# Another order table for an attention and feed-forward kernel on one core

## The chip, the cores and the metric

The kernel runs on one core of a Trainium2 chip. Five instruction streams run side by side: TensorE (PE in the profile, with its weight loads as PEld) for matrix products, VectorE (DVE), ScalarE (ACT) and GpSimd (POOL) for elementwise work, and SyncE (SP), which here only issues DMAs; POOL issues DMAs too, and ACT three. Each stream works through its instructions in the order in which they were built, and waits at an instruction until what it depends on is done. The metric is the device time of one execution in microseconds, and the time of a kernel is the median over its runs.

## What is computed

64 heads (8 batches of 8), 576 positions of 64 values, attention by feature maps, then a feed-forward layer that takes the largest of three products:

```python
def phi(x):
    proj = np.einsum('bhsd,df->bhsf', x, w_phi)
    proj = proj - np.max(np.abs(proj), axis=-1, keepdims=True)
    return np.concatenate([np.exp(proj), np.exp(-proj)], axis=-1)
q_p, k_p = (phi(q), phi(k))
kv = np.einsum('bhsf,bhsd->bhfd', k_p, v)
z = np.sum(k_p, axis=2)
num = np.einsum('bhsf,bhfd->bhsd', q_p, kv)
den = np.einsum('bhsf,bhf->bhs', q_p, z)[..., None] + 1e-06
x = (num / den)                                  # heads side by side: 4608 rows of 512
h = np.maximum(np.maximum(x @ w1, x @ w2), x @ w3)   # 768 wide
out = h @ w_out
```

## The kernel before

The attention is cut into 16 units of four heads, the feed-forward layer into nine chunks: one per batch (512 rows each), and a ninth for the 64 last positions of all batches.

A unit goes through these steps. Queries and keys are loaded and cast by POOL's DMAs into `qk_bf` (four buffers), the last positions of the queries by SP's into `tail_raw`, the values by SP's into `v_raw` (four buffers, which the first keys and, at the end, partial sums use as well). The loads become transposed blocks in `qkT`: for units 0 to 3 on TensorE (`tps`, L508, copied out by DVE or ACT at L519 and L521), from unit 4 on by two DMA transposes on SP (L527), one for the keys and one for the queries. TensorE projects: `psk`, `pst` and `psq` (L545) for the maxima, which DVE takes (L549), `psm` (L642, and L650 for the last positions) for the queries' exponentials. ACT makes the exponentials `Ek` (L553) and `Eq` (L633). From the keys' maxima ACT makes `em` (L591), and POOL multiplies the values with it into `vab` (L597), about 2 us a product and two to a unit. TensorE forms `kvps` from `Ek` and `vab` (L616), 72 products a unit (for units 0 and 1 in two halves of 36), and `psn` (L683); DVE scales and adds (L692, L695), takes reciprocals (L740), POOL divides into `x_sb` (L741), and a DMA transpose on SP (L773) turns that into `xT` (units 0 and 1 on TensorE).

The weights w1, w2, w3 and w_out are loaded by four DMAs on POOL's queue (L952). TensorE transposes w1 into `pwT` (L1008) and multiplies it with w_out (`pm`, L1018); POOL subtracts w1 from w2 and w3 in six steps (L982). A chunk then has the products `ups` (L891), the comparisons on DVE (L901) and ACT (L905), and the products `ops` (L924, L929), copied out by ACT or DVE (L939) and stored by SP (L943). Chunks 6 to 8 use a form with seven products instead of eight (`ups` at L820, sums on DVE at L829 and L864). One piece of chunk 7 is stored in two parts, of 384 and of 128 columns, by ACT.

All of this is made as 1687 steps, each with its dependencies and buffers. Which step stands where is not found by the program: the string `PLAN` lists all steps, in the order in which they are built. A word such as `262S0@42.1` names the step (262), its engine (T for TensorE, D, A, G for POOL, S for SyncE), the buffer of its tile among those of its kind, if it takes one (0), and a start in microseconds. The order of the words is what counts. No engine waits for the start that stands in a word; before 30 us `fill` uses it for one thing: where the listed starts leave TensorE a gap, it puts products of no use (`idler`, L1066) into it, as many as fit beside the uses of the PSUM banks. For a step that two engines can do, such as a copy, the letter also decides which does it.

```python
for word in PLAN.split():
    what, start = word.split("@")
    at = next(i for i, c in enumerate(what) if c.isalpha())
    n, slots = nodes[int(what[:at])], iter(what[at + 1:])
    n.eng, n.start = ENGINES[what[at]], float(start)
    ...
    order.append(n)
```

Of the kernel before, what the change touches and what calls it, by code (L numbers as in the profile page):

```python
# [90 lines left out]
103G0@1.2 3A@0.7 1D@0.8 4A@1.3 10S0@0.7 12D1@4.0 11A@4.0 5D@4.2 0G@1.9 19T0@4.5 20A0@4.9 6D@4.4 29T12@5.5 32D0@6.0 9G@2.5 8G@3.2  # L91
35D@6.6 31A0@6.8 102G@3.9 260G2@4.6 16S0@1.1 104G@8.1 17G@8.3 186G3@8.6 185G@9.3 259G@10.0 1166G@10.7 13S@2.5 7A@7.2 106T3@7.4 33A0@7.5
34A@8.0 30A@8.4 107D1@8.1 119T45@8.8 122D1@9.3 187S1@2.9 124A1@9.2 123A1@9.7 112T67@9.1 115D@9.9 110T0@9.4 111A@10.2 114A@10.6
120A@11.1 121A@11.6 25T2@10.0 15D@10.5 14D@10.7 27T1@10.9 21T3@11.1 118D@10.9 26D@11.5 28D@11.8 43T04@12.2 73T21@12.3 22D@12.0
23T3@12.7 125D@12.4 113A@12.1 46D@13.0 47D0@13.3 18S1@4.3 24D@13.6 116A@12.6 76A0@13.0 45A@13.5 1169G@11.5 54A0@13.8 75A0@14.0
117A@14.4 1167G@12.2 74A@14.9 36T56@13.1 108T4@13.8 42D@14.0 39D@14.6 109D@15.2 38A@15.4 77A@15.9 41A@16.4 58A@16.8 51T37@15.1 52D@15.8
44A@17.0 126T24@15.9 130D1@16.4 105S2@5.0 131T13@16.5 333G1@13.6 129D@16.7 53D@17.0 133D@17.6 57G0@14.3 55G@14.5 2G@15.6 56G@15.8
188G@16.9 128A@17.3 37A@17.6 137A1@18.0 40A@18.2 78T0@17.5 62T47@17.8 80A@18.7 64A0@19.0 132D@18.2 48T35@18.4 50D@18.8 63D@19.4
49D@19.6 60G@17.2 61G@18.3 138G1@18.4 59G@19.5 127A@19.1 79A@19.4 68T67@19.3 134T15@19.6 263T4@19.9 190T3@20.4 135D@20.2 65T20@21.0
71A@19.7 69A@20.2 72A@20.7 70A@21.2 141A@21.6 67A@21.8 139G@20.6 334S0@8.7 142G@22.0 261G@23.1 140G@23.3 81A0@22.0 136D@20.8 191D2@21.4  # L100
264D3@22.0 192T1@21.6 85T76@22.1 86D0@22.6 66A@22.2 193A@22.3 1168G@23.5 82T05@22.4 161T3@22.7 83D@23.0 90T47@23.2 151T21@23.6
163A1@23.2 162A1@23.5 87D@23.4 93T03@23.9 265T6@24.2 84D@23.8 91D1@24.2 94D@24.6 404G0@24.2 88D0@25.1 92D@25.2 145T54@24.8 153A@24.0
155A@24.5 154A@25.0 152A@25.5 146A1@25.9 164A1@26.1 147A@26.3 194T0@25.5 1188T7@25.7 156T12@26.3 195A@26.4 144G@24.4 335G@24.6
337S0@35.1 95D@25.6 266D@26.0 1189D0@26.6 165T54@26.6 168T03@26.9 143G@24.8 166D2@27.1 169D@27.5 148T67@27.3 167D@27.9 96D1@28.4
149D@28.5 170D@28.7 189S3@36.5 1192T5@28.0 158A@26.7 403G@25.9 159A@27.2 157A@27.7 160A@28.1 262S0@42.1 150A@28.6 1190T0@28.4
1191D@29.1 171D2@29.7 1193A@28.8 89G0@26.6 332G@27.8 97G@28.6 301T46@29.0 176T31@29.3 173T27@29.6 1198T0@29.9 177D0@29.9 174D@30.2
178D@30.6 175D@31.1 179D0@31.6 304A0@29.7 305A0@30.1 302A@30.6 303A@31.1 196T53@31.3 1199A@31.6 276T21@31.6 98T7@31.9 402G@29.8
267T6@32.1 100T4@32.3 199D0@31.8 279D1@32.4 101D@33.0 268D@33.4 99D@33.6 172G1@30.6 281A0@32.0 1200T0@32.5 181T4@33.8 197A0@32.5
277A1@33.1 198A1@33.6 1201A@34.1 180G@31.9 203T67@34.2 183T5@34.5 1196T0@34.8 202D@34.0 182D@34.6 206D@35.0 406S1@42.8 338S@45.5
184D@35.6 291T45@36.2 208A@34.6 207A@35.1 278A@35.6 209D@36.0 292D0@36.6 293D@37.2 282D@37.9 204A@36.1 201A@36.6 205A@37.0 200A@37.5  # L110
1194T2@36.5 1195A@38.0 1197A@38.5 1171G@33.6 1172G@35.7 1170G@37.8 210T74@37.9 215T56@38.0 214D1@38.5 216D@38.8 280A@39.0 213D@39.4
1210T3@38.4 1173G@39.9 217D@39.7 1174G@42.0 1175G@44.1 269T20@39.3 288T45@39.5 1211A1@39.5 271A@39.9 270A@40.4 212A@40.9 273A@41.1
211A@41.6 289D@40.3 290D@40.9 274A@41.9 1206T1@40.1 1208T6@40.9 1214T3@41.8 272D@41.5 1207D@42.1 283T74@42.8 228T52@42.9 1215A@42.9
1209D@42.7 275D@43.3 287D@43.9 1204T1@43.2 230A1@43.4 229A1@43.8 1205D@44.3 1212T3@44.1 218T60@45.0 306T45@45.2 231A@44.3 285A@44.8
221A0@45.0 284A@45.2 222G0@46.5 1218T1@45.6 1213D@45.1 220D@45.7 286D@46.3 219D@46.7 1219D@47.3 309A@45.7 224A@46.1 310A@46.3 307A@46.7
294A1@47.2 308A@47.4 232A@47.9 1226T3@46.4 223G@48.5 1227D@47.9 1224T0@47.3 1225D@48.5 233T76@48.2 241A0@48.4 235A@48.7 353T15@48.5
475S1@47.7 1216T4@48.7 357D1@49.1 234A@49.2 339T23@49.6 238T0@49.9 356D0@49.4 1217D@49.8 225T57@50.5 345D@50.4 342D@51.0 236A@49.6
# [980 lines left out]
```

## Time and profile before

| | |
|---|---|
| median of three runs | 275.77 us (275.74 to 277.81) |
| the profiled execution | 276.54 us, its span 274.7 us |
| granted TensorE clock, mean over the span | 0.993 |
| moved by DMA | 44.54 MB, of it 34.64 MB read and 9.44 MB written in HBM |
| issues, median to landing | values 5.4 us (16), keys 6.9 us (15), queries 7.3 us (15), stores of 256 KB 3.0 us (31) |

The profile is of one execution. Its time stands 1.84 us above its span, which runs from the first to the last instruction of the program. Rows of instructions give the start, the time taken, the engine, the line, the operation with its tile, and how many instructions were merged; in brackets stands the engine's idle time before the row and what ended it. "x36" after a row is a count. Rows of DMA issues give what is moved, the queue, the count, the size, and the median time from issue to landing.

### The profile page before, as it was taken

The page shows a single profiled execution, that of the slowest core. Times are in us where ns is not written, and L with a number is a line of the kernel's source. Part 1 is how long each engine was busy: PE and PEld are TensorE (multiplying, and loading weights), DVE is VectorE, ACT ScalarE, POOL GpSimd, SP SyncE. Part 2 cuts the span into 40 slices and gives each one's busy share as a digit, 9 for nine tenths or more (in the row PEclk, how much of TensorE's full clock was granted, in tenths as well). Part 3 has the DMA queues.
Part 4 walks back from the last instruction along what each step waited for, and adds up shares of the span by engine and source line. Part 5 has one row for each costly group of instructions (what it writes and reads, how often), then busy time and mean ns, then how long its engine had stood idle before and what let it go on. Part 6 is the DMA issues. An engine that isn't in the chain of part 4 may idle for free.

```text
span 274.7 us, 8748 instructions
## 1 busy us (share of the span) xinstructions
PE 265.6 (97%) x3540; PEld 159.8 (58%) x3540; DVE 241.5 (88%) x489; ACT 214.2 (78%) x516; POOL 186.9 (68%) x183
## 2 busy tenths in 40 slices
PE   7789999999999999999999999999999999999994
PEld 4458744566565556565655455655548766686652
DVE  3799999999999888988888998999898999998871
ACT  3999999999999999779878989799987443254241
POOL 6798999999769951987569279937899856600000
PEclk9989999999999999999999999999999999999999
DMA  6999999999999999999999994596505053020253
GB/s 143 258 220 209 210 195 242 249 175 193 193 195 160 262 178 254 212 217 204 180 201 164 240 216 70 108 248 156 128 6 161 2 98 115 0 76 4 47 154 144
DMA packets 76200, 44.54 MB, mean 162 GB/s; under 512 B 52672, under 2 KB 67328, under 8 KB 76160
## 3 DMA queue, kind: packets, MB, share of 16 engines
q1 hardware_dynamic: 60880, 31.93, 53.6%
q0 software_dynamic: 14912, 11.77, 29.1%
q8 instruction: 27, 0.44, 0.6%
q10 hardware_dynamic: 368, 0.30, 0.3%
q14 instruction: 13, 0.11, 0.1%
HBM read 34.64 MB, written 9.44 MB: 160 GB/s over the span
## 4 chain that ended last, share of the span: by engine, by line
PE 89%; DVE 4%; ACT 3%; DMA 2%; issue 0%; POOLq 0%
PE ups L891 21%; PE ops L929 17%; PE ops L924 12%; PE ups L820 10%; PE psn L683 8%; PE kvps L616 7%; PE psm L642 3%; PE psq L545 3%; PE psk L545 3%; DMA qk_bf<-in_k_dram 2%; PE pm L1018 2%; ACT Eq L633 2%; DVE mk L549 2%; PE tps L508 1%; ACT Ek L553 1%; PE pst L545 1%
## 5 line engine op out<-in xcount | busy, mean ns | idle before, releaser
L633 ACT ACTIVATE Eq<-psm 128x512 bf16<-128x512 f32 (+1 forms) x160 | 81.7, 579 | 6.7 <-PE psm L642 6.1
L597 POOL TENSOR_TENSOR vab<-v_raw,em 128x1152 bf16<-128x1152 f32 (+1 forms) x36 | 68.3, 1906 | 17.5 <-ACT em L591 17.4
L553 ACT ACTIVATE Ek<-psk 128x512 bf16<-128x512 f32 x128 | 71.6, 641 | 2.2 <-DVE mk L549 1.2
L891 PE MATMUL ups<-xT,w_bf 128*128 128x512 bf16 x288 | 69.7, 380 | 0.0
L741 POOL TENSOR_TENSOR x_sb<-y,rden 128x640 bf16<-128x640 f32 x32 | 39.7, 1252 | 20.8 <-DVE rden L740 20.1
L929 PE MATMUL ops<-wout_bf,hT 128*128 128x512 bf16 (+2 forms) x222 | 52.0, 374 | 0.0
L549 DVE TENSOR_REDUCE mq<-psq 128x4 f32<-128x512 f32 x64 | 41.2, 681 | 4.8 <-PE psq L545 4.6
L549 DVE TENSOR_REDUCE mk<-psk 128x4 f32<-128x512 f32 x64 | 42.2, 681 | 2.2 <-PE psk L545 1.4
L891 PEld LDWEIGHTS <-w_bf 128*128 128x128 bf16 x288 | 25.0, 98 | 26.3 <-issue 1.3
L692 DVE TENSOR_TENSOR y<-psn,sq 128x325 f32<-128x325 f32 x64 | 30.6, 492 | 3.9 <-PE psn L683 3.1
L929 PEld LDWEIGHTS <-hT 128*128 128x128 bf16 x222 | 20.7, 98 | 21.7 <-DVE hT L864 0.5
L683 PEld LDWEIGHTS <-Eq 128*128 128x128 bf16 x640 | 26.1, 98 | 11.4 <-issue 2.3
L695 DVE TENSOR_TENSOR y<-y,psn 128x325 f32<-128x325 f32 x64 | 30.2, 487 | 2.1
L939 ACT COPY osb<-ops 128x512 f32<-128x512 f32 (+2 forms) x29 | 16.9, 582 | 17.2 <-PE ops L929 16.8
L829 DVE TENSOR_TENSOR parts<-ups,parts 128x512 f32<-128x512 f32 (+1 forms) x45 | 29.1, 679 | 1.1 <-PE ups L820 0.8
L683 PE MATMUL psn<-kv_sb,Eq 128*128 128x65 bf16 x640 | 28.7, 194 | 0.4 <-ACT Ek L553 0.4
L545 PEld LDWEIGHTS <-qkT 64*128 64x128 bf16 x576 | 18.6, 95 | 16.2 <-issue 12.3
L901 DVE TENSOR_TENSOR hT<-hT,ups 128x512 bf16<-128x512 bf16 x36 | 23.9, 676 | 2.0 <-PE ups L891 1.3
L924 PE MATMUL ops<-xT 128*128 128x512 bf16 x96 | 24.6, 381 | 0.0
L862 ACT ACTIVATE hT<-hT 128x512 bf16<-128x512 bf16 x18 | 10.8, 628 | 16.5 <-DVE hT L829 16.5
L616 PE MATMUL kvps<-vab,Ek 64*128 64x65 bf16 x1152 | 22.0, 192 | 0.0
L616 PEld LDWEIGHTS <-Ek 64*128 64x128 bf16 x1152 | 20.5, 96 | 1.0 <-issue 0.2
(84 smaller groups left out, 391.5 us busy)
## 6 DMA issues: line engine op xcount, KB each, us to landing
v_raw<-in_v_dram SPq DMA_DIRECT2D x16, 576.0 KB, 5.4
out_dram<-osb SPq DMA_DIRECT2D x31, 256.0 KB, 3.0
qk_bf<-in_k_dram POOLq DMA_DIRECT2D x15, 288.0 KB, 6.9
qk_bf<-in_q_dram POOLq DMA_DIRECT2D x15, 256.0 KB, 7.3
w_bf<-in_moe_w_dram POOLq DMA_DIRECT2D x3, 768.0 KB, 15.7
tail_raw<-in_q_dram SPq DMA_DIRECT2D x16, 64.0 KB, 4.6
out_dram<-osb SPq DMA_DIRECT2D x8, 128.0 KB, 2.3
wout_bf<-in_moe_w_out_dram POOLq DMA_DIRECT2D x1, 768.0 KB, 18.7
```

Source lines behind the costliest of these rows:

```text
L545: nc.tensor.matmul(ps[s]()[:, i, :], lhsT=qkT()[r, n, :], rhs=wph[r, :], start=True, stop=True)
L549: return nd(kind, {"DVE": 0.598 if n == 4 else 0.331}, lambda: nc.vector.tensor_reduce(dst(m()), ps()[:, 0:n, :], AXX, ALU.max, apply_abso ...
L553: return nd("ek", {"ACT": 0.478 if n == 4 else 0.264}, lambda: nc.scalar.activation(dst(Ek[g]()), ps()[:, 0:n, :], EXP, scale=1.0 - 2.0 * ...
L597: made.append(chosen(n_, lambda n_, g=g, t0=t0, t1=t1: (nc.vector if n_.eng == "DVE" else nc.gpsimd).tensor_tensor(vab()[:, g, t0:t1, 0:D] ...
L616: nc.tensor.matmul(kvps[ab]()[:, pr, g, :], lhsT=Ek[g]()[r, t, :], rhs=vab()[r, g, t, :], start=(pr == prs[0] and g + j == 0), stop=(pr == ...
L633: return nd("eq", {"ACT": 0.478 if n == 4 else 0.264}, lambda: nc.scalar.activation(Eq[g]()[:, t0:t0 + n, :], ps()[:, 0:n, :], EXP, scale= ...
L683: nc.tensor.matmul(psn[g]()[:, i, :], lhsT=Eq[g]()[:, t, :], rhs=kv()[:, pr, ab, g, :], start=True, stop=True)
L692: n_ = nd("xu", {"DVE": 0.064 + 0.0676 * n_t}, lambda: nc.vector.tensor_tensor(yv(y()), ps(0), sq_of(sq()).unsqueeze(len(shape) - 1).to_br ...
L741: divs[pr] = nd("x", {"POOL": 1.2}, lambda pr=pr, y=y, rden=rden: nc.gpsimd.tensor_tensor(x_sb()[:, pr].rearrange("p t a d -> p a t d"), y ...
L891: nc.tensor.matmul(ups()[:, o * n:(o + 1) * n], lhsT=w_bf[i + (not plain)][:, ct, jj * P:(jj + 1) * P], rhs=tokens_of(ct)[:, cols] if halv ...
L924: nc.tensor.matmul(ops_()[:, 0:hi - lo], lhsT=tile_of(ct, tt), rhs=line_w[c_i > MOVE][:, ct, lo:hi], start=(ct == 0), stop=False)
L929: nc.tensor.matmul(ops_()[:, 0:hi - lo], lhsT=hT()[:, j, tt * P:(tt + 1) * P], rhs=wout_bf[:, j, lo:hi], start=plain and j == 0, stop=(j = ...
```

## The change

`PLAN` is replaced; nothing else is. Step numbers stay what they are, so every step has the same work, and TensorE has the same products of use. The first words and two later ones:

```diff
-103G0@1.2 3A@0.7 1D@0.8 4A@1.3 10S0@0.7 12D1@4.0 11A@4.0 5D@4.2 0G@1.9 19T0@4.5 20A0@4.9 6D@4.4 29T12@5.5 32D0@6.0 9G@2.5 8G@3.2
...
+3A@0.7 103G0@1.2 9G1@1.9 1D@0.8 4A@1.3 10S0@0.7 12A@4.0 6D@3.7 7D@3.9 0G@2.6 11A@4.3 8G@3.2 2G@3.9 102G@4.1 16S0@1.1 17G@8.1 104G@8.3
```

Thirty-eight steps change their engine, among them ten copies of `ops`, nine of `kvps` and six first steps of the comparison, between DVE and ACT in both directions. The idle products rise from 42 to 47. Three places are shown as the built program has them; the numbers behind the names are the program's own and differ between the two.

TensorE, where unit 1's first-half queries have been projected, or (after) unit 0's second half. `psq` are projections, `idler` the products of no use, `psm` and `kvps` what follows. Before:

```order
L545 LDWEIGHTS qkT_189
L545 MATMUL psq_364<-wph_69,qkT_189 128x128
L1066 LDWEIGHTS idle_68
L1066 MATMUL idler_389<-idle_68 128x256
L1066 LDWEIGHTS idle_68
L1066 MATMUL idler_391<-idle_68 128x256
L650 LDWEIGHTS wph_69
L650 MATMUL psm_393<-qkT_125,wph_69 128x256
L616 LDWEIGHTS Ek0_185
L616 MATMUL kvps_395<-vab_377,Ek0_185 128x65
```

After:

```order
L1066 MATMUL idler_390<-idle_68 128x256
L1066 LDWEIGHTS idle_68
L1066 MATMUL idler_392<-idle_68 128x256
L1066 LDWEIGHTS idle_68
L1066 MATMUL idler_394<-idle_68 128x256
L1066 LDWEIGHTS idle_68
L1066 MATMUL idler_396<-idle_68 128x256
L1066 LDWEIGHTS idle_68
L1066 MATMUL idler_398<-idle_68 128x256
L1066 LDWEIGHTS idle_68
L1066 MATMUL idler_400<-idle_68 128x256
L642 LDWEIGHTS wph_69
```

Six idle products stand where two stood, and what follows is unit 0's `psm` instead of the last positions' and `kvps`, which come later. Ahead of this piece, behind the second four query transposes of unit 0, stand now three idle products, eight `psq`, eight transposes, one idle product and eight `psq`; further ahead, twelve idle products stand in a row before unit 0's last key transposes, where six were spread among them.

POOL's queue at the start, where queries, keys and weights are loaded and cast (`ident` and `wph_low` are constants, `tail_raw` the last positions). Before:

```order
L432 DMA qk_bf_84<-in_q_dram 128x2x256 x2
L432 DMA qk_bf_77<-in_q_dram 128x4x256
L442 DMA qk_bf_150<-in_k_dram 128x2x576
L479 CAST qk_bf_77<-tail_raw_152 128x2x64
L479 CAST qk_bf_84<-tail_raw_152 128x2x64
L442 DMA qk_bf_157<-in_k_dram 128x2x576
L432 DMA qk_bf_157<-in_q_dram 128x4x256
```

After:

```order
L432 DMA qk_bf_80<-in_q_dram 128x2x256
L379 MEMSET wph_low_70 64x128
L432 DMA qk_bf_78<-in_q_dram 128x4x256
L479 CAST qk_bf_80<-tail_raw_97 128x2x64
L479 CAST qk_bf_78<-tail_raw_97 128x2x64
L442 DMA qk_bf_102<-in_k_dram 128x2x576
L442 DMA qk_bf_104<-in_k_dram 128x2x576
L432 DMA qk_bf_104<-in_q_dram 128x4x256
```

The keys of unit 3 (`qk_bf_150` before, `qk_bf_102` after) are issued behind the two casts of the last positions, no longer ahead of them.

SyncE from unit 4's key transpose on (`qkT_715` and `qkT_565` are unit 4's, `qkT_971` and `qkT_1299` unit 5's). Before, with the values of units 2, 3, 6 and 4 in this order:

```order
L527 DMA_TRANSPOSE qkT_715<-qk_bf_372 128x10x128
L484 DMA v_raw_792<-in_v_dram 128x2x576
L484 DMA v_raw_808<-in_v_dram 128x2x576
L527 DMA_TRANSPOSE qkT_971<-qk_bf_643 128x10x128
L527 DMA_TRANSPOSE qkT_715<-qk_bf_372 128x8x128
L484 DMA v_raw_1183<-in_v_dram 128x2x576
L475 DMA tail_raw_1286<-in_q_dram 64x4x64 x2
L527 DMA_TRANSPOSE qkT_971<-qk_bf_643 128x8x128
L484 DMA v_raw_1333<-in_v_dram 128x2x576
```

After, with the values of units 2, 3, 4 and 8 in this order:

```order
L527 DMA_TRANSPOSE qkT_565<-qk_bf_376 128x10x128
L484 DMA v_raw_716<-in_v_dram 128x2x576
L527 DMA_TRANSPOSE qkT_565<-qk_bf_376 128x8x128
L484 DMA v_raw_974<-in_v_dram 128x2x576
L484 DMA v_raw_1046<-in_v_dram 128x2x576
L527 DMA_TRANSPOSE qkT_1299<-qk_bf_561 128x10x128
L484 DMA v_raw_1301<-in_v_dram 128x2x576
L475 DMA tail_raw_1303<-in_q_dram 64x4x64 x2
L527 DMA_TRANSPOSE qkT_1299<-qk_bf_561 128x8x128
```

Unit 4's queries (128x8x128) have moved ahead of the values of unit 3, and the values of units 4 and 8 stand where those of units 6 and 4 stood. Further down, the values of unit 10 are issued ahead of those of unit 6, and those of unit 13 soon behind those of unit 7, and most stores of chunks 0 to 3 change places. At the end the last piece's 384 columns are copied by ACT and stored first, and its 128 columns are copied by DVE and stored last.

296 lines of the change are left out of this document (148 added, 148 removed).

## The prediction, made before the changed kernel had run

> **What bounds the kernel now.** I read the page first, then the busy time by stretches, then TensorE's rows around the few places where it is not full. The page's first two lines give the span and TensorE's share:
>
> ```profile
> span 274.7 us, 8748 instructions
> ...
> PE 265.6 (97%) x3540; PEld 159.8 (58%) x3540; DVE 241.5 (88%) x489; ACT 214.2 (78%) x516; POOL 186.9 (68%) x183
> ```
>
> By stretches (busy us of PE, PEld, DVE, ACT and POOL with their counts, then the granted clock, the DMA share and GB/s):
>
> ```profile
> 30.00:50.00 20.00, 20.00 (x196) 9.98 (x193) 19.85 (x42) 19.94 (x48) 19.83 (x12) 1.00 1.22 222
> 50.00:60.00 10.00, 9.65 (x243) 6.58 (x238) 9.97 (x21) 10.00 (x32) 9.37 (x9) 1.00 1.01 207
> 60.00:220.00 160.00, 160.00 (x2355) 92.74 (x2354) 143.90 (x300) 140.23 (x342) 120.62 (x109) 1.00 0.92 171
> ...
> 270.00:274.70 4.70, 0.69 (x5) 0.20 (x2) 0.00 (x0) 0.48 (x1) 0.00 (x0) 0.95 0.32 113
> ```
>
> From 60 to 220 us TensorE is never empty: 160.00 of 160. The new table gives TensorE the same products and only reorders them, so there nothing is to be gained, and a loss needs a wait that TensorE does not have now. What can move is the head before 30 us, the narrow place at 50 to 60 us (0.35 us of TensorE idle, with ACT at 10.00 of 10 and DVE at 9.97), and the last store.
>
> **The head: the clock.** Four stretches in a row, cut where the granted clock changes:
>
> ```profile
> 11.40:14.81 3.41, 2.88 (x34) 1.85 (x35) 3.41 (x10) 3.40 (x10) 2.14 (x3) 1.00 1.13 295
> 14.81:18.23 3.42, 2.65 (x30) 1.22 (x30) 3.42 (x8) 3.42 (x11) 3.42 (x7) 1.00 1.25 210
> 18.23:21.64 3.41, 3.35 (x60) 2.50 (x60) 2.95 (x6) 2.88 (x10) 3.41 (x5) 0.50 1.33 205
> 21.64:25.05 3.41, 3.35 (x90) 2.94 (x88) 3.11 (x7) 3.31 (x12) 2.64 (x5) 1.00 1.19 209
> ```
>
> The stretch with the least TensorE work (2.65 us, 30 products, 1.22 us of weight loads) is followed by one at half clock, in which TensorE is nearly full (3.35 of 3.41), so that its slowness counts. The same pieces at full and at half clock, from the timeline, and two groups of idle products:
>
> ```profile
> 5.73 0.83 PE L1066 MATMUL idler<-idle 128*128 128x256 bf16 x6
> ...
> 8.02 0.49 PE L1066 MATMUL idler<-idle 128*128 128x256 bf16 x3
> ...
> 15.62 0.40 PE L545 MATMUL psq<-wph,qkT 64*128 64x128 bf16 x8
> ...
> 17.92 1.41 PE L616 MATMUL kvps<-vab,Ek 64*128 64x65 bf16 x36
> 19.11 0.64 PE L545 MATMUL psq<-wph,qkT 64*128 64x128 bf16 x8
> ...
> 20.13 0.61 PE L642 MATMUL psm<-qkT,wph 64*128 64x512 bf16 x2
> 20.51 0.66 PE L545 MATMUL psq<-wph,qkT 64*128 64x128 bf16 x8
> ...
> 22.34 0.75 PE L616 MATMUL kvps<-vab,Ek 64*128 64x65 bf16 x36
> ...
> 25.06 0.39 PE L642 MATMUL psm<-qkT,wph 64*128 64x512 bf16 x2
> ```
>
> Half clock cost 1.41 - 0.75 = 0.66 on kvps, 0.24 and 0.26 on the two psq, and 0.61 - 0.39 = 0.22 on psm: 1.4 us. In the new order TensorE has, in the place of the thin stretch (behind the second four query transposes of unit 0), three idle products, eight psq, eight transposes, one idle product, eight psq, six idle products and two psm. Without the first three, which should still fall before 14.81, that is 33 products, seven of them idle ones, where 30 with fewer idle ones were; the stretch before it had 34 and was not followed by half clock. So I expect the clock to stay up. The twelve idle products that now stand ahead of unit 0's last key transposes cost (0.83 - 0.49)/3 = 0.11 each, 1.3 us in all; they cost the path nothing if those transposes wait anyway for VectorE's and ScalarE's casts, and at worst 1.3 us.
>
> [...]
>
> **How much of 1.4 us passes on.** Next behind the head stand the weights. Issue, time to landing, and first user of w1 (transposed on TensorE) and of w2 (POOL's subtractions):
>
> ```profile
> 10.55 0.77 POOL L952 DMA_DIRECT2D w_bf<-in_moe_w_dram  x1
> ...
> 12.10 0.80 POOL L952 DMA_DIRECT2D w_bf<-in_moe_w_dram  x1
> ...
> w_bf<-in_moe_w_dram POOLq DMA_DIRECT2D x1, 768.0 KB, 15.7
> ...
> w_bf<-in_moe_w_dram POOLq DMA_DIRECT2D x1, 768.0 KB, 21.6
> ...
> 27.08 0.61 PE L1008 MATMUL pwT<-ident,w_bf 128*128 128x128 bf16 x8
> ...
> 34.62 10.45 POOL L982 TENSOR_TENSOR w_bf<-w_bf 128x1024 bf16<-128x1024 bf16 x5
> ```
>
> w1 lands at 10.55 + 15.7 = 26.25 and is used at 27.08: room of 0.8 us. w2 lands at 33.70 and is used at 34.62: room of 0.9 us. So at most 0.9 us can pass. The new POOL order issues unit 3's keys later and puts one cast between w1 and wout. I cost that at nothing, since w2 spends 21.6 us in a queue that is busy ahead of it; if that cover is gone, w2 lands later by about one issue, 0.8 us, which takes the room away. Behind it POOL, ACT and TensorE meet:
>
> ```profile
> 47.12 6.26 POOL L597 TENSOR_TENSOR vab<-v_raw,em 128x1152 bf16<-128x1152 f32 x3
> ...
> 55.98 0.44 PE L683 MATMUL psn<-kv_sb,Eq 128*128 128x65 bf16 x9 [0.35 <-ACT Ek L553]
> ```
>
> POOL runs without a gap from 34.62 through the subtractions to these products; TensorE waits for ACT at 55.98. A gain arrives only if all three are early. Between 0 and 0.9 I take the middle, 0.5 us, since ACT, already full at 50 to 60 us, has to make it up as well.
>
> **SyncE behind unit 4's first transpose.** Before, the queue has unit 4's keys, the values of units 2 and 3, unit 5's keys, and then unit 4's queries. After, unit 4's queries stand ahead of unit 3's values, which are followed at once by unit 4's values, so unit 3's values wait behind a transpose that itself waits for its load. Issues, and times to landing (unit 4's query load, unit 4's keys, unit 2's values, unit 3's, unit 4's queries):
>
> ```profile
> 29.01 0.80 POOL L432 DMA_DIRECT2D qk_bf<-in_q_dram  x1
> ...
> 35.31 2.90 SPq L527 DMA_TRANSPOSE qkT<-qk_bf  x1
> 38.26 1.09 SPq L484 DMA_DIRECT2D v_raw<-in_v_dram  x2
> 40.48 4.35 SPq L527 DMA_TRANSPOSE qkT<-qk_bf  x1
> ...
> qk_bf<-in_q_dram POOLq DMA_DIRECT2D x1, 256.0 KB, 13.6
> ...
> qkT<-qk_bf SPq DMA_TRANSPOSE x1, 9.8
> ...
> v_raw<-in_v_dram SPq DMA_DIRECT2D x1, 576.0 KB, 8.4
> ...
> v_raw<-in_v_dram SPq DMA_DIRECT2D x1, 576.0 KB, 9.2
> ...
> qkT<-qk_bf SPq DMA_TRANSPOSE x1, 6.7
> ```
>
> The query load lands at 29.01 + 13.6 = 42.6, and the transpose can start then. It took 6.7 us when it started at 44.8 (40.48 + 4.35), so it lands at 49.3; the values of unit 3 landed 1.4 us behind those of unit 2 (38.9 + 9.2 = 48.1 against 38.26 + 8.4 = 46.7), so they now land at 50.7. POOL first needs them with the third product of its row, at 47.12 + 2 x 2.09 = 51.3. The margin is 0.6 us (0.1 with the gain above): price 0. From the other side, a transpose as slow as that of unit 4's keys, 9.8 us, lands at 52.4, the values at 53.8, and POOL is 2.5 us late. Being early there gains nothing, since POOL is busy until 51.3. I take 0, for it stands nearest in the queue to the 6.7.
>
> **The rest.** The other moved loads (early values of units 8, 10 and 13, late stores) have their cover in POOL, idle for 39 of the 160 us, and in the stores, for which nobody waits before the end; the cost of each is 0 unless one holds the queue past the POOL's idle time, then about one transfer. About thirty steps change engine, nearly as many from ScalarE to VectorE as back; both have idle time in 60 to 220 us (16 and 20 us), which hides it. At the end the last chunk's two pieces change places: 384 columns first, 128 last.
>
> ```profile
> 269.14 0.27 ACT L939 COPY osb<-ops 128x128 f32<-128x128 f32 x1 [1.04 <-PE ops L929]
> ...
> 270.72 0.48 ACT L939 COPY osb<-ops 128x384 f32<-128x384 f32 x1 [1.31 <-PE ops L929]
> ...
> out_dram<-osb ACTq DMA_DIRECT2D x1, 192.0 KB, 2.2
> out_dram<-osb ACTq DMA_DIRECT2D x1, 64.0 KB, 2.8
> ```
>
> The last copy is 0.2 us shorter; its transfer took 0.6 longer, though beside others. Between -0.2 and +0.4 I take 0.
>
> **The sum.** The profiled execution took 276.54 us around a span of 274.7; with -0.5 it is 276.0. The median of the runs shown, 275.77, lies 0.77 lower, so the time comes to 275.3 us.
>
> **The rivals.**
> Nothing is gained: the clock drops all the same, a window later or earlier, or ACT keeps the pace at 55.98. For it speaks that ACT is full there and that 33 products against 30 is little; against it, that seven idle products now stand there. 275.8 us, and up to 277.1 if twelve idle products in a row do delay what follows (+1.3).
> Slower: unit 3's values land at 53.8, behind a transpose of 9.8 us. POOL stands still for 2.5 us, and TensorE with it, since the kvps of unit 3 need POOL's product: 275.8 + 2.5 = 278.3. TensorE, so idle, can drop to half clock once more, 1.4 us: 279.7. I take 279.0, between them. It decides once the transpose takes more than 7.3 us from 42.6. For it speaks the 9.8 of the transpose before it; against it the 6.7 of this very one.
> Faster by more: all 0.9 us, the wait of 0.35 at 55.98, and 0.2 at the end: 274.3.
>
> **How the numbers follow.** Forecast (275.3) 0.45, nothing gained 0.33, slower by the values 0.14, faster by more 0.06, something that no row shows 0.02. The range from 274.2 to 277.4 holds the first two and the fourth, and leaves out the slow case; the likeliest one's own is 274.8 to 275.7. One per cent, about what a measurement of this kernel tells from no change, is 2.8 us: below 273.0 no case reaches, 0.02 for the unseen; above 278.5 lies most of the slow case, and I count it there whole, 0.14; between them 0.45 + 0.33 + 0.06 = 0.84.
>
> **What would show it.** Right: granted clock 1.00 from about 5 us on; w1's first transpose at 26.3 to 26.9; POOL's first subtraction before 34.6; TensorE without idle time from 60 to 220 us; unit 3's values landed by 51. Wrong: a stretch at 0.50 behind 15 us, a wait of POOL for v_raw near 51 us, or any wait of TensorE past 60 us.

## The result and the profile after

The changed kernel is slower: 278.7 us (276.83 to 281.64, 20 runs) against 275.77 (275.2 to 277.81, 20 runs), a ratio of 1.0088 with a 95% interval from 1.0066 to 1.0111. The ratio is estimated from the fast runs alone, 19 and 20, and is not the quotient of the two medians. The prediction had 275.3 and a range up to 277.4. The profiled execution took 279.32 us around a span of 276.5.

The time by stretches, with the columns of the prediction's rows (busy us of PE, PEld, DVE, ACT and POOL with counts, granted clock, DMA share, GB/s), after:

```profile
14.81:18.23 3.42, 3.20 (x38) 1.96 (x39) 3.42 (x7) 3.42 (x11) 3.40 (x7) 1.00 1.29 197
18.23:21.64 3.41, 3.36 (x113) 3.01 (x110) 3.41 (x7) 3.41 (x14) 3.41 (x5) 1.00 1.30 207
23.73:27.14 3.41, 1.82 (x55) 1.42 (x53) 2.50 (x6) 2.51 (x9) 3.39 (x5) 1.00 1.24 210
27.14:30.55 3.41, 3.39 (x63) 2.66 (x64) 2.66 (x8) 2.27 (x6) 2.47 (x4) 0.50 1.17 210
...
60.00:220.00 160.00, 160.00 (x2350) 92.34 (x2349) 145.35 (x303) 138.82 (x342) 123.16 (x115) 1.00 0.89 168
220.00:240.00 20.00, 19.45 (x133) 12.54 (x131) 19.86 (x34) 6.71 (x13) 11.69 (x11) 1.00 0.31 86
240.00:270.00 30.00, 29.63 (x200) 19.42 (x200) 26.88 (x49) 11.81 (x21) 0.00 (x0) 1.00 0.23 68
```

and the last two stretches before:

```profile
220.00:240.00 20.00, 19.89 (x134) 12.66 (x132) 19.69 (x36) 7.10 (x13) 12.73 (x15) 1.00 0.28 73
240.00:270.00 30.00, 30.00 (x209) 19.82 (x208) 24.93 (x45) 12.05 (x22) 0.00 (x0) 1.00 0.27 79
```

Between 5 and 270 us the granted clock of the kernel before changes only at 18.23 and 21.64 us; the prediction's other cuts are no changes of it. The thin stretch is gone: from 14.81 to 21.64 the clock is 1.00 where it was 0.50 for half of it. But TensorE is busy for only 1.82 us of the 3.41 from 23.73 to 27.14, and the half clock comes then, with TensorE full (3.39). From 60 to 220 us TensorE is full as before. Behind 220 us it loses 0.44 and 0.37 us that it did not lose before.

One profile is one run. The mean granted clock is on record for the changed kernel's 20 runs and for 129 runs of the old kernel taken beside the experiments. One stretch of 3.41 us at half clock takes 0.006 off it (3.41 x 0.5 / 274.7). Of the old kernel's runs 87 had 0.996 or more, with a median of 275.81 us; 37 had 0.990 to 0.994, with a median of 276.46, and five less. Of the changed kernel's runs ten had 0.998 or more, with a median of 277.64, and ten 0.994 or less, with a median of 279.4. So the half clock comes and goes from run to run in both kernels, the new order has not removed it, and without it the changed kernel is still 1.8 us slower.

**The first place.** TensorE's timeline after, around the idle time, and POOL's first subtraction (L982):

```profile
24.91 0.27 PE L650 MATMUL psm<-qkT,wph 64*128 64x256 bf16 x1
25.16 0.56 PE L1008 MATMUL pwT<-ident,w_bf 128*128 128x128 bf16 x7
27.16 0.29 PE L1008 MATMUL pwT<-ident,w_bf 128*128 128x128 bf16 x1 [1.44 <-issue]
27.38 0.61 PE L642 MATMUL psm<-qkT,wph 64*128 64x512 bf16 x2
...
35.70 2.12 POOL L982 TENSOR_TENSOR w_bf<-w_bf 128x1024 bf16<-128x1024 bf16 x1
```

TensorE came to w1's first transposes at 25.16 us, 1.9 us earlier than before (27.08); w1 had landed at 25.11. It ran seven of eight, stood for 1.44 us, and ran the eighth. "issue" means that nothing in the profile holds it: the eighth transpose and its weight load wait for no semaphore. Counting TensorE's matmuls and weight loads from the start, exactly 700 lie ahead of the stall. The DMA part of the profile shows what can be missing. Whole execution, then the two stretches from 22.0 to 24.7 and from 24.79 to 25.77 us:

```profile
q8 instruction: 27, 0.44, 0.7%
...
q0 software_dynamic: 463, 0.56, 118.7%
...
q8 instruction: 1, 0.02, 6.3%
```

The profile has a queue that it calls instruction, with 27 packets of 16,384 bytes. In the first stretch none of them moved, and POOL's loads filled the DMA engines; in the second one did, which kept one engine of 16 busy throughout (6.3%). TensorE went on 1.38 us behind that packet's end. That these are TensorE's instructions is my reading: the profile does not say what is in a packet, but the count fits, 27 packets for 7090 matmuls and weight loads, one for every 263. The experiments below bear it out.

**The second place.** VectorE and POOL at 230 to 236 us, after, and two of TensorE's waits:

```profile
231.98 1.36 DVE L864 TENSOR_TENSOR hT<-hT,parts 128x512 bf16<-128x512 bf16 x1
233.26 1.37 DVE L799 TENSOR_TENSOR sums<-xT 128x512 bf16<-128x512 bf16 x1
234.56 1.37 DVE L864 TENSOR_TENSOR hT<-hT,parts 128x512 bf16<-128x512 bf16 x1
...
231.90 1.16 POOL L799 TENSOR_TENSOR sums<-xT 128x512 bf16<-128x512 bf16 x1
233.14 1.22 POOL L799 TENSOR_TENSOR sums<-sums,xT 128x512 bf16<-128x512 bf16 x1
234.31 1.33 POOL L799 TENSOR_TENSOR sums<-xT 128x512 bf16<-128x512 bf16 x1
...
234.69 0.61 PE L820 MATMUL ups<-sums,w_sums 128*128 128x256 bf16 x4 [0.29 <-DVE sums L799]
240.44 0.61 PE L820 MATMUL ups<-sums,w_sums 128*128 128x256 bf16 x4 [0.37 <-ACT osb L939]
```

and before, where POOL waited for VectorE's sum:

```profile
231.52 0.41 DVE L799 TENSOR_TENSOR sums<-sums,xT 128x512 bf16<-128x512 bf16 x1
231.86 1.71 DVE L864 TENSOR_TENSOR hT<-hT,parts 128x512 bf16<-128x512 bf16 x2
...
232.02 1.26 POOL L799 TENSOR_TENSOR sums<-xT,sums 128x512 bf16<-128x512 bf16 x1 [1.39 <-DVE sums L799]
```

A sum of two tiles in SBUF took VectorE 0.41 us while POOL stood still (231.52, before), and 1.36 or 1.37 while POOL ran sums of its own (after). After, each of VectorE's three ends 0.28 us behind the end of the POOL sum that began just before it (233.34 behind 233.06, 234.64 behind 234.35, 235.93 behind 235.65). The table had changed the engines of chunk 8's second and third sum, so that POOL no longer waits and its seven sums run back to back. That POOL's sums hold VectorE's up is tested below; by what means, no trace shows.

### The profile page after: what moved, and what is told of

The parts are those of the page before. It is cut to its first block, busy times and chain, and to the rows that moved or that the text cites. A ratio compares the mean times of both kernels' runs of the same rounds, so it can differ in the third digit from the quotient of the medians.

```text
span 276.5 us, 8768 instructions
## 1 busy us (share of the span) xinstructions
PE 266.9 (97%) x3545; PEld 161.3 (58%) x3545; DVE 244.0 (88%) x491; ACT 211.6 (77%) x512; POOL 187.8 (68%) x185
## 5 line engine op out<-in xcount | busy, mean ns | idle before, releaser
L891 PEld LDWEIGHTS <-w_bf 128*128 128x128 bf16 x288 | 25.2, 98 | 27.2 <-issue 1.3
L939 ACT COPY osb<-ops 128x512 f32<-128x512 f32 (+1 forms) x27 | 16.1, 598 | 14.6 <-PE ops L929 11.8
L924 PE MATMUL ops<-xT 128*128 128x512 bf16 x96 | 24.8, 380 | 0.0
```

What stands on the lines that cost most here:

```text
L891: nc.tensor.matmul(ups()[:, o * n:(o + 1) * n], lhsT=w_bf[i + (not plain)][:, ct, jj * P:(jj + 1) * P], rhs=tokens_of(ct)[:, cols] if halv ...
L924: nc.tensor.matmul(ops_()[:, 0:hi - lo], lhsT=tile_of(ct, tt), rhs=line_w[c_i > MOVE][:, ct, lo:hi], start=(ct == 0), stop=False)
```

## Experiments

Ratios are against runs of the old kernel on the same chip. Where a diff shows words of the table, only their places, engines and tile numbers matter.

**What stops TensorE at 25.7 us.** w1's transposes moved behind the next three products:

```diff
-161T5@25.1 1188T3@25.3 152A@24.1 ... 156T21@25.9 ... 1189D0@26.3 165T06@26.4 168T54@26.7 ... 148T73@27.1
+161T5@25.1 152A@24.1 ... 156T21@25.3 ... 165T06@25.7 168T54@26.2 ... 1188T3@26.6 1189D0@26.3 148T73@27.1
```

> The changed kernel, with w1's first transposes (L1008) and their copy moved behind the three products that followed them; nothing else. In the changed kernel's trace TensorE ran seven of the eight transposes from 25.16 us, stood for 1.44 us, ran the eighth at 27.16, and then had half the clock from 27.14 to 30.55. Theory 'landing' (w1's last part had not arrived): TensorE has other work now, the idle 1.44 us at 25.7 is gone, the clock stays at 1.00 behind 27 us, and the time falls by 1.0 us or more, to 277.5 (ratio to before 1.005). Theory 'instructions' (TensorE had run out of fetched instructions: the eighth weight load waited for no semaphore): the idle time of 1.3 to 1.6 us stays where it was, between 25.3 and 27.3 us and behind the 705th matmul or weight load, on L683's products in place of the transposes; time within 0.5 us of 278.7.

Measured: 279.43 us (4 runs), ratio 1.0132 (1.0087 to 1.0178). It decides nothing. In its profile half clock lay from 14.83 to 21.66, so TensorE came to the place with 700 ahead only at 28.46 us, 1.41 behind the end of the packet, and hardly stood there; and the edit brought a wait of its own, the kvps behind the transposes for the copy of their bank:

```profile
PE kvps L616 <- DVE hT L1011: 1.1, 1, 1.1
```

(This expectation and the next three count 705, with five entries of the queue that are neither matmul nor weight load; the later ones count 700.)

Next, wider idle products, which are fewer:

```diff
-                best = None
+                best, d, wide = (None, 2 * d, 2) if t + 2 * d <= n.start - 0.12 else (None, d, 1)
...
-            nc.tensor.matmul(idler[:, 0:2 * P], lhsT=idle, rhs=idle.unsqueeze(1).to_broadcast([P, 2, P]), start=True, stop=True)
+            nc.tensor.matmul(idler[:, 0:2 * P * wide], lhsT=idle, rhs=idle.unsqueeze(1).to_broadcast([P, 2 * wide, P]), start=True, stop=True)
```

> The changed kernel, with its idle products twice as wide (512 columns) wherever two would fit, so that 25 stand for 47 and 44 matmuls and weight loads fewer lie ahead of 25 us; nothing else. Theory 'instructions': the 705th of TensorE's matmuls and weight loads is now 44 further on in the program, some 1.2 us of work; the instruction packet still lands near 25.8, so the idle 1.44 us shrinks to 0 to 0.4, the clock is 1.00 from 27.1 to 30.5, POOL's first subtraction (L982) starts by 34.8 in place of 35.70, and the time falls by 0.8 to 2.0 us, to some 277.3. Theory 'landing': the idle 1.44 us at w1's first transposes stays, and the time too (278.7, within 0.5).

Measured: 277.63, ratio 1.0057 (1.0027 to 1.0087). The stall at w1 is gone, the clock is 1.00 to the end, and the eight transposes ran through from 25.12, though w1 had landed at 25.07, hardly earlier than in the changed kernel (25.11): the landing is refuted. But a stall of 0.60 us had opened at 209 us, in the middle of a kvps. The same edit on the old kernel (22 idle products for 42):

> The old kernel with idle products twice as wide wherever two fit (22 for 42); nothing else. Theory 'instructions': the old kernel's TensorE gets to its 705th matmul or weight load at 28.1 us, behind its supply, so 40 fewer ahead of it win nothing: 275.9 within 0.5. Rival 'wider idle products keep the clock up better, whatever the instructions': 0.5 to 1.4 us faster than the old kernel, and fewer runs at a clock below 0.997.

Measured: 277.09, ratio 1.0034 (1.0011 to 1.0057): neither theory, it got slower. Its timeline shows a stall at 150 us (and, not explained, a wait of 0.74 us at 210 for VectorE's `kv_sb`); the kernel with both repairs (below) has the like of the stall at 211 us:

```profile
148.79 1.12 PE L616 MATMUL kvps<-vab,Ek 64*128 64x65 bf16 x60
150.74 0.37 PE L616 MATMUL kvps<-vab,Ek 64*128 64x65 bf16 x12 [0.83 <-issue]
```

```profile
207.85 2.40 PE L616 MATMUL kvps<-vab,Ek 64*128 64x65 bf16 x140
210.98 0.24 PE L616 MATMUL kvps<-vab,Ek 64*128 64x65 bf16 x4 [0.73 <-issue]
```

With forty matmuls and weight loads fewer at the start, every place in the count lies later in the work, all the way to the end. The stalls over 0.3 us, with the times of the packet of the instruction queue ahead of each, from the records of the traces that are complete up to there:

| kernel | matmuls and weight loads ahead | as 256 n + r | packet ends | TensorE goes on | behind it by |
|---|---|---|---|---|---|
| changed | 700 | 2, 188 | 25.77 | 27.15 | 1.38 |
| sums repaired | 700 | 2, 188 | 25.30 | 26.85 | 1.55 |
| old end | 700 | 2, 188 | 25.79 | 27.21 | 1.42 |
| changed, 26 more ahead | 700 | 2, 188 | 24.60 | 26.18 | 1.58 |
| sums and head repaired | 700 | 2, 188 | 25.83 | 27.08 | 1.25 |
| SyncE repaired | 700 | 2, 188 | 26.52 | 28.10 | 1.58 |
| old, 24 more ahead | 701 | 2, 189 | 25.80 | 27.11 | 1.31 |
| old, narrow | 956 | 3, 188 | 30.08 | 31.54 | 1.46 |
| old, wide | 4281 | 16, 185 | 149.20 | 150.74 | 1.54 |
| both repairs | 6071 | 23, 183 | 209.58 | 210.98 | 1.40 |

All ten stand at nearly the same remainder of 256, and at exactly the same one, 193, when the few other entries of TensorE's queue (four to ten by then) are counted too. So I take a packet to hold 256 entries and the stalls to stand where one begins; that is an estimate from the remainders and from the one packet for every 263 above, for no trace shows what a packet holds. TensorE went on 1.25 to 1.58 us behind the packet's end. Near 27 us the entry in question is the one with 705 ahead; in none of the 19 profiles does it begin less than 1.25 us behind the end of its packet, whether TensorE had to wait or not. The old kernel ran from its 444th to its 700th between 22.6 and 27.9 us, with its packet from 25.17 to 26.06; the changed kernel wanted its 700th at 25.5, having passed its 444th at 20.8, with the packet from 24.79 to 25.77. In the first, 256 took 5.3 us, in the second 4.7, and the packet came little earlier.

Three tests move this boundary. The old kernel with idle products half as wide, and more of them:

```diff
-                d = 0.22 if t < COLD else 0.11
+                d = 0.11 if t < COLD else 0.055
...
-            nc.tensor.matmul(idler[:, 0:2 * P], lhsT=idle, rhs=idle.unsqueeze(1).to_broadcast([P, 2, P]), start=True, stop=True)
+            nc.tensor.matmul(idler[:, 0:P], lhsT=idle, rhs=idle, start=True, stop=True)
```

> The old kernel with idle products half as wide (128 columns) and 89 of them in place of 42, so that 94 more matmuls and weight loads lie ahead of 30 us; the same idle time is filled. Theory 'instructions': the 705th of them now stands some 1.5 to 2.5 us earlier in the old kernel's program, TensorE reaches it at 26 us or before, and stands there with no semaphore to wait for, for 0.5 to 1.8 us, until some 27.2; the time is 0.5 to 2 us longer than the old kernel's. Rival (the stall belongs to the changed kernel's order or to w1's load): no idle time of that kind, time within 0.4 of the old kernel's.

Measured: 277.79, ratio 1.0059 (1.0031 to 1.0086). The size was right, the place wrong: nothing stood at the 700th, since the packets had come earlier too (12.97 us for 16.41, then 23.02 for 25.17); 0.38 us stood at the 956th, at 31.54. What else the kernel lost, its profile does not show. Then only the idle products ahead of 3.9 us cut in two, in the old kernel and in the changed one:

```diff
-                d = 0.22 if t < COLD else 0.11
+                d, cols = (0.11, 1) if t < 3.9 else (0.22 if t < COLD else 0.11, 2)
```

> The old kernel, with the first 12 idle products (ahead of 3.9 us, before any data is there) cut into 24 of half the width; the same time is filled, everything behind them is the same, only 24 matmuls and weight loads more lie ahead of it. In ten traces so far every stall without a semaphore stands at the 183rd to 190th matmul or weight load of a row of 256, and ends 1.3 to 1.55 us behind the end of a 16 KB instruction packet. Theory 'rows of 256': the stretch from the 444th to the 700th now begins and ends 24 earlier in the program, where the old kernel runs through 256 in 4.5 us in place of 5.3, while a packet takes 4.9 to 5.7 us from the moment the stretch begins to the moment TensorE can go on; so TensorE stands 0.3 to 1.1 us at its 700th, inside a kvps (L616), with no semaphore; 0.2 to 1.2 us slower than the old kernel. Rival 'idle products and instructions do not matter': no stall there, within 0.3 us of the old kernel.

Measured: 276.58, ratio 1.0023 (0.9999 to 1.0047). The profile has a wait of 0.39 us at 27.11 and puts it down to VectorE's y. But that instruction had ended at 26.75, 0.36 us earlier. The transpose that waited is the entry with 705 ahead (701 matmuls and weight loads, four others) and began 1.31 us behind the end of its packet: it is the expected stall, at the low end of its range. What it costs the kernel is not clear of zero.

> The changed kernel with its first 13 idle products cut in two the same way: 26 matmuls and weight loads more ahead of the rest, nothing else. Theory 'rows of 256': the stall leaves w1's transposes and stands 26 earlier in the program, inside the kvps before them (L616), still the 700th, and is longer: 1.6 to 2.2 us in place of 1.43, since the 256 ahead of it are run through in 4.2 us in place of 4.9; 0.3 to 1.0 us slower than the changed kernel (ratio to the old one 1.010 to 1.013). Theory 'w1's landing': the stall stays with the eighth transpose of w1.

Measured: 279.08 (6 runs), ratio 1.0129 (1.0093 to 1.0165). TensorE's timeline:

```profile
24.72 0.67 PE L616 MATMUL kvps<-vab,Ek 64*128 64x65 bf16 x31 [0.46 <-POOL vab L597]
26.18 0.26 PE L616 MATMUL kvps<-vab,Ek 64*128 64x65 bf16 x5 [0.79 <-issue]
...
26.49 0.62 PE L1008 MATMUL pwT<-ident,w_bf 128*128 128x128 bf16 x8
```

The stall left the transposes, which now run as eight, and stands 26 instructions earlier in the program, in the kvps. That settles what it is: it goes with the count and not with the work. It was 0.79 us, not 1.6, since this packet came at 23.70; its size is a race between two times, and I had fixed one of them. That the time lies in the expected range is luck, for the stall that was to make it longer was half as long as in the changed kernel.

**The sums at 230 us.** Engines and order of chunk 8's second and third sum as in the old kernel:

```diff
-1610G3@226.8 1611G@227.9 1613G@228.9 ... 1476D@228.7 1503A@227.7 ... 1504D@230.0 1612D@230.3 1485D@230.7
+1610G3@226.8 1612G@230.3 ... 1476D@228.7 1611D@227.9 1613G@228.9 1503A@227.7 ... 1504D@230.0 1485D@230.7
```

> The changed kernel, with the second and third sum of chunk 8 (L799) on the engines they had before: one from POOL to VectorE, one from VectorE to POOL, in the old kernel's order on VectorE; nothing else. Theory 'end': VectorE's sums of two SBUF tiles (L864, L799) took 1.36 to 1.37 us in place of 0.41 while POOL ran its own sums; POOL now waits for VectorE's sum, VectorE runs two of its three meanwhile at 0.41 to 0.45, one stays slow, TensorE's waits at 234.7, 236.0 and 240.4 us (0.29, 0.25 and 0.37) fall below 0.4 together, and the time falls by 0.5 to 1.3 us, to some 277.8. Rival: the end is late because all before it is late, the engines make no difference: 278.7 within 0.4.

Measured: 277.26, ratio 1.0034 (1.0002 to 1.0065). VectorE's rows are the old kernel's again, one slow sum in place of three:

```profile
230.51 0.41 DVE L799 TENSOR_TENSOR sums<-sums,xT 128x512 bf16<-128x512 bf16 x1
230.84 1.71 DVE L864 TENSOR_TENSOR hT<-hT,parts 128x512 bf16<-128x512 bf16 x2
```

None of the three waits of TensorE is left in its timeline. The reverse, the changed kernel's engines in the old kernel:

```diff
-1510T@226.0 1612G@228.1 1474D@225.7 ... 1495D@229.0 1611D@229.6 1511A3@227.5 ... 1504D@230.0 1485D@230.3
+1510T@226.0 1611G@229.6 1474D@225.7 ... 1495D@229.0 1511A3@227.5 ... 1504D@230.0 1612D@228.1 1485D@230.3
```

> The old kernel with the changed kernel's engines for the second and third sum of chunk 8 (L799): the one on POOL directly behind the first, the other on VectorE between the two sums L864; nothing else. Theory 'end': POOL no longer waits 1.39 us, its seven sums run back to back, and three of VectorE's sums of two SBUF tiles take 1.36 in place of one; 1.0 to 1.5 us slower than the old kernel. Rival (it was the changed order around the sums, not the engines): within 0.4 us of the old kernel.

Measured: 277.04, ratio 1.0043 (1.0025 to 1.0062), 1.2 us slower. Two sums took 1.37, the third 0.55, and TensorE waited for the one in the middle:

```profile
233.64 1.05 PE L820 MATMUL ups<-sums,w_sums 128*128 128x256 bf16 x8 [1.33 <-DVE sums L799]
```

Undone in one kernel and done in the other, the two letters are worth 1.2 to 1.4 us.

**Are these two places all?** The changed table up to the word `1017G@201.4`, then the old one's order and engines for all that is left:

```diff
 1145T6@204.8 1017G@201.4
-1146A@205.1 1147A@205.4 1066T27@205.0 ...
+1351S@156.9 1177G@186.8 1130G@198.7 1026S@203.3 ...
```

> The changed kernel's order and engines up to some 203 us of the trace, and from there the old kernel's order and engines for all that is left. Theory 'two places' (1.0 us lost at the instruction stall ahead of 31 us, some 1.0 lost from 228 to 240 us, 0.4 won at the very end): 278.7 - 1.0 + 0.4 = 278.1, from 277.6 to 278.5. Theory 'head alone': the loss ahead of 31 us is all of it, and the old end gives back only the 0.4: 278.7 to 279.2. Theory 'end alone': the stall in the head is made up in the slack behind it, and the time comes back to 275.8 to 276.3.

Measured: 277.7, ratio 1.0065 (1.0037 to 1.0093): within theory 'two places', and slower than the old kernel by 1.8, so the end is not all. The other way round:

```diff
 1026S@203.3 1061G@203.2
-1187G0@205.2 1179G@206.3 1436T0@202.7 ...
+1315S@142.5 1602G@147.4 1607G@180.8 1183G0@189.8 ...
```

> The old kernel's order and engines up to some 203 us, and from there the changed kernel's for all that is left. Theory 'two places': the sums cost 1.2 to 1.4 (the old kernel with only their engines exchanged was 1.2 slower), and the changed tail is worth 0 to 0.6: 275.85 + 1.3 - 0.3 = 276.8, from 276.2 to 277.3. Theory 'head alone': 275.5 to 276.0.

Measured: 281.42 (6 runs), ratio 1.0207 (1.0181 to 1.0233). This is the join, not the end: TensorE stood for 2.94 us right behind it, for a copy by ScalarE. It says nothing about the two theories.

```profile
208.28 0.39 PE L642 MATMUL psm<-qkT,wph 64*128 64x512 bf16 x2 [2.94 <-ACT osb L939]
```

Both repairs, the wide idle products and the old sums:

> The changed kernel with both repairs: idle products twice as wide wherever two fit (25 for 47), and the two sums of chunk 8 back on their old engines. Theory 'two places' (instruction stall in the head, slow sums at 228 to 236 us): the two gains add, since they lie 200 us apart: 278.7 - 1.1 (wide idle products alone gave 277.63) - 1.4 (sums alone gave 277.26) = 276.2, from 275.0 to 276.6, with no idle time of TensorE over 0.6 us from 20 to 30 us and one slow sum on VectorE in place of three. Rival 'one slack' (what the head gains is waited away at the same later point that the sums' gain fills): 277.0 to 277.4.

Measured: 277.66, ratio 1.0045 (1.0019 to 1.0072), 1.5 more than hoped. The wide products had cost what they won: the stall of 0.73 at 211 us (above), and half clock from 15.80 to 19.21 behind a stretch with 1.95 us of TensorE in 3.41. So a repair that leaves both alone: wide products ahead of 12 us only, which takes 34 matmuls and weight loads away, and three products with w_out near 90 to 115 us in halves, which puts 36 back.

```diff
-                best = None
+                best, cols = None, 4 if t < 12 and t + 2 * d <= n.start - 0.12 else 2; d *= cols // 2
...
-                        nc.tensor.matmul(ops_()[:, 0:hi - lo], lhsT=hT()[:, j, tt * P:(tt + 1) * P], rhs=wout_bf[:, j, lo:hi],
-                                         start=plain and j == 0, stop=(j == JT - 1))
+                        for c0, c1 in ((lo, lo + 256), (lo + 256, hi)) if c_i == 1 and tt < 3 else ((lo, hi),):
+                            nc.tensor.matmul(ops_()[:, c0 - lo:c1 - lo], lhsT=hT()[:, j, tt * P:(tt + 1) * P], rhs=wout_bf[:, j, c0:c1], start=plain and j == 0, stop=(j == JT - 1 and c1 == hi))
```

With the old sums:

> The changed kernel with three repairs: the two sums of chunk 8 on their old engines; idle products ahead of 12 us twice as wide where two fit (34 matmuls and weight loads fewer ahead of the stall, the products that keep the clock up behind 12 us untouched); and three of chunk 1's products with w_out (L929, near 90 to 115 us) cut into halves of 256 columns, which puts 36 back, so that the later rows of 256 begin where they did in the changed kernel. Theory 'rows of 256': the stall at the 700th falls from 1.43 (1.02 in the kernel with the sums alone) to 0 to 0.5, none comes at 207 to 211 us, and the time is 276.3 to 277.0 (sums alone: 277.26). Rival 'the head does not reach the end': 277.2 to 277.6.

Measured: 276.56, ratio 1.0012 (0.9983 to 1.0040): within the range, though the interval overlaps that of the sums alone. In the profile 0.36 us of the stall are left, and none is at 209 us. That profile is of the longest of the 12 runs (279.47), in which TensorE also waited 2.18 us for `xT` at 101 us. The same without the sums:

> The changed kernel with the head's repair alone (idle products ahead of 12 us twice as wide where two fit, and three of chunk 1's products with w_out cut into halves further on, so that 34 matmuls and weight loads fewer lie ahead of the stall and as many as before ahead of 200 us); the two sums stay where the change put them. Theory 'two places': the stall of 1.43 falls below 0.5, three slow sums (1.36 each) stay on VectorE, and the time lies where the sums alone leave it, 276.5 + 1.3 = 277.4 to 278.1 (ratio to the old kernel 1.004 to 1.008). Theory 'sums alone' (what the stall costs is made up later): 278.4 to 279.0.

Measured: 277.75, ratio 1.0061 (1.0021 to 1.0100): inside what was expected, though its interval overlaps the changed kernel's. The profile has no stall at all, but another wait: 1.0 us at 99 us, for `xT`. And with the old end:

> The changed kernel up to some 203 us with the head's repair, and the old kernel's order and engines for all behind it: neither stall nor slow sums. Theory 'two places': nothing of the loss is left but the two kernels' own tails, 276.0 to 277.0 (ratio 1.000 to 1.004), within 0.5 of the kernel that has the changed tail with the sums repaired (276.56). Theory 'a third place between 31 and 203 us': 277.3 to 278.0, as with the old end alone (277.70).

Measured: 276.9, ratio 1.0012 (0.9977 to 1.0048). The same wait is there, 1.3 us.

**The third place.** SyncE's rows in the kernel with the head repaired (the transpose of unit 5's x is the L773), then, of `xT` from 84 to 101 us, who waits for it (us in all, and how often) and the landings of the two transposes in that stretch, unit 4's and unit 5's:

```profile
89.83 1.00 SPq L484 DMA_DIRECT2D v_raw<-in_v_dram  x1
90.92 0.43 SPq L943 DMA_DIRECT2D out_dram<-osb  x1
91.45 1.96 SPq L773 DMA_TRANSPOSE xT<-x_sb  x1
93.46 1.08 SPq L484 DMA_DIRECT2D v_raw<-in_v_dram  x1
```

```profile
  PE ups L891: 1.0, 1
...
DMA to landing us min/median/max: 5.2/6.4/7.6
```

In the old kernel the last row reads

```profile
DMA to landing us min/median/max: 3.5/4.2/4.9
```

It is 4.3/5.6/6.9 in the changed kernel, where TensorE came late enough not to meet it. Unit 5's transpose is the 7.6 here, the 6.9 in the changed kernel, and the 3.5 in the old one; the 4.9 there, which the expectations below take for it, is unit 4's. The new order put a load of values, 576 KB, on each side of unit 5's transpose. Both moved away, with sums and head repaired:

```diff
-401S@84.3 ... 615S@87.0 544S3@88.4 1239S@89.1 ... 470S@91.5 961S1@93.0 ... 963S3@104.8
+401S@84.3 544S3@88.4 ... 615S@87.0 1239S@89.1 ... 470S@91.5 ... 963S3@104.8 961S1@93.0
```

> The changed kernel with head and sums repaired, and two of SyncE's issues moved: unit 7's values from one place ahead of the transpose of unit 5's x into xT (two, with a store between) back to directly behind unit 4's, where the old kernel had them, and unit 13's values from directly behind it to behind unit 13's key transpose; nothing else. In the last two profiles that transpose took 7.6 and 8.0 us to landing (4.9 in the old kernel, 6.9 in the changed one) with a load of values on each side of it, and TensorE waited 1.0 and 1.3 us for it at 99 us (L891), which gave back half of what the head's repair had won. Theory 'SyncE': it lands within 6 us, TensorE's wait at 99 us is below 0.3, and the time falls by 0.7 to 1.3 from 276.56, to 275.3 to 275.9 (ratio 0.995 to 1.000). Rival 'made on POOL' (x itself is late): the wait stays, 276.3 to 276.9.

Measured: 275.95 against 275.93, ratio 0.9999 (0.9974 to 1.0024), which lies in the expected range; the step from 276.56 is 0.6, a little less than expected, and the two intervals overlap. No wait of TensorE over 0.3 us is left behind 15 us, and unit 5's transpose, now the shorter of the two, lands after 4.4:

```profile
DMA to landing us min/median/max: 4.4/4.7/5.0
```

> The same two moves on SyncE, in the kernel with the head's repair and the old kernel's order from 203 us. Theory 'SyncE': 276.9 - 1.1 = 275.8, from 275.3 to 276.2 (ratio 0.996 to 1.000), no wait over 0.3 at 99 us. Rival: 276.6 to 277.2.

Measured: 276.6, ratio 1.0020 (0.9991 to 1.0048), within the rival's range. The wait is gone, but nothing is gained: the ratio was 1.0012 before.

> The changed kernel with the same two moves on SyncE alone; stall and slow sums stay. Theory 'hidden': TensorE comes to 99 us 2.6 us later than in the repaired kernel, behind the transpose's landing, so nothing is won: 278.4 to 279.0. Rival 'SyncE's order costs by itself': 277.3 to 278.0.

Measured: 277.67 (6 runs), ratio 1.0054 (1.0034 to 1.0074): here the rival was right. The two moves win about 1 us by themselves, at the edge of what the intervals tell apart (1.0066 to 1.0111 in the changed kernel). How they do it is not shown: one profile of the changed kernel has TensorE full at 99 us, which does not mean that its other runs had.

With all three repaired, the changed kernel's time is the old one's. The three together account for the loss, and the share of the sums is shown both ways; how the rest divides between the stall and the transpose is not shown. No version beat the old kernel.

## Why the prediction was wrong

- **TensorE full from 60 to 220 us, nothing gained or lost.** Full it was, 160.00 of 160. But "nothing lost" rested on the old kernel's landings; the third place lay inside, covered by the late head.
- **The head's clock.** Right in the profiled run as far as 21.64, with TensorE 1.9 us earlier at w1, but as a property of the order wrong: ten of the changed kernel's 20 runs had half clock, 42 of the old one's 129. The first rival, with the clock dropping all the same, was the better answer to this. The twelve idle products delayed nothing that shows.
- **How much passes on: 0.5 of 0.9.** This step failed first. I bounded the gain by w1 and w2 and took a value between 0 and the bound. w1 was there at 25.1; what bounded it was the next 256 instructions, which no term had. The sign was wrong with it: the stall emptied a stretch, half clock followed in the profiled run, and POOL's first subtraction started at 35.70, not before 34.6. The profiles show the stall's part: with stalls of 0.79 and 1.02 us and no half clock the subtraction started at 34.14 and 34.08, with neither (head repaired) at 33.13 and 33.39. How much of this reaches the end is not clear: the head's repair took 0.7 us off beside the repaired sums (276.56 for 277.26) and 1.0 alone, both within the runs' spread, and among runs at a clock of 0.996 or more nearly nothing alone (277.51 in seven runs for 277.64 in ten), which fits the 1.0 us that TensorE then waited at 99 us.
- **The sum, 276.0 less 0.77.** Also wrong. The 0.77 us by which the profiled run stood above the median were taken off beside the 0.5 to be won from the half clock. But most of the 0.77 is the half clock: the old kernel's runs with one such stretch took 276.46, those without 275.81. Two runs in three had none, and the median with them, so there was nothing to win from it.
- **SyncE behind unit 4's transpose, price 0.** Right where I looked: unit 4's query transpose took 4.8 us, and POOL did not wait for values near 51. The slow rival's 279.0 lies close to the time measured, but nothing of it happened.
- **The other moved loads, price 0.** Failed. The cover that I named, POOL idle for 39 us, is the cover of who reads the values. Who was hurt is the transfer beside them: the transpose of unit 5's x, 3.5 us in the old kernel, 6.9 and 7.6 here. Two moves were worth some 1.0 us alone, 0.6 behind the other repairs, neither clear of the runs' spread.
- **Thirty-eight engine changes, price 0.** Failed, and the largest piece, 1.2 to 1.4 us, shown in both directions. The term weighed ScalarE against VectorE alone; six of the 38 steps move to or from POOL, and two of these six are the sums. "Both have idle time in 60 to 220 us" says nothing of 228 to 236, where seven POOL sums stand in a row; the price of a sum depends on what runs beside it, 0.41 or 1.36, and the row with 1.71 for two was in the profile before.
- **The end, 0.** Not separated: old and new end differ by nothing measurable once sums and head are repaired (both 1.0012).

## What to carry to other kernels

When a table moves work, price each step by what runs beside it at its new place, not by its engine's share of idle time: a two-input sum on VectorE took 1.36 us beside GpSimd's sums for 0.41 without, and the transpose of unit 5's x 6.9 us between two loads of values for 3.5 in the old kernel. Count instructions where products are tiny. Here the packet for the next row of 256 began to move 2.6 and 4.0 us after TensorE had passed the boundary before. The changed kernel ran through its row in 4.7 us and stood for 1.44 at its end; the old one took 5.3 and did not stand. With 26 matmuls and weight loads of idle products more at the front, the stall, then of 0.79 us, stood 26 earlier in the program, and with 40 fewer one of 0.83 us stood in the old kernel at 150 us, which had none before. Before a stretch at half clock is counted as time to be won, ask how many of the runs behind the median have it. A gain early in the program is worth what the next fixed time behind it lets through; look for the second and third such time before pricing the first.

## What the hardware showed

After TensorE had passed the boundary with 444 ahead, the next packet began to move 2.6 us later in the old kernel (22.6 to 25.2) and 4.0 in the changed one (20.8 to 24.8), while POOL's loads of keys, queries and weights filled the DMA engines (share 1.21 and 1.18); it took 0.9 to 1.0 us, and the changed kernel's TensorE went on 1.38 behind it. In the old kernel with wide idle products one packet waited for 6.7 us at 140 to 147 us (share 1.32), and ahead of the stall at 211 us one waited for 0.6 (share 0.59). That busy DMA engines make it wait would agree with these numbers, but I did not try it. Eleven of the 19 traces have such a stall, of 0.36 to 1.44 us.

The half clock wanders from profile to profile: it began at 18.23 in the old kernel's, at 27.14 in the changed one's, at 14.2 to 15.8 in six others and at 17.8 in one, in two only behind 100 us, and in eight not at all before the kernel's end. A stall of 1.44 us was followed by it (the changed kernel), one of 1.02 was not (sums repaired). Single runs of one kernel differ by more than some of the repairs are worth, which is why only the sums' share and the total are certain.
